# A new order of the small pieces between attention units, and a rearranged start, in a kernel that is attention times a gated MLP

## The chip, the cores and the metric

One NeuronCore of a Trainium2 chip, one launch. The metric is the time on the device in microseconds (us). Lower is better.

## The reference

All tensors are bf16; S = 2048 tokens, D = 1024, 32 heads of 32, F = 3584.

```python
xn  = layernorm(x)                                # (x - mean) / sqrt(var + 1e-5)
s   = attention(xn @ wqkv, 32 heads) @ wo         # softmax over 2048 keys
y   = layernorm(xn)
g   = silu(gelu_tanh(y @ w1 + b1) @ w2 + b2)
out = x + s * g
```

## The kernel before

The main work is 512 *attention units*. One unit takes 4 heads, 256 keys and 256 queries: scores on TensorE, two exponentials of 128x1024 on ScalarE, and P times V (with a row sum beside it) on TensorE, one unit later. From unit 7 on every unit also gets one piece of *other* work for TensorE from a hand-ordered list, `PLAN`:

```python
PLAN = """
q a a v a a a . a v a v a v a a a q a q a q a v q v a a a a q a a q ...   # 517 entries
"""
# a   w1 for 128 of F, one chunk of tokens (352 or 320 wide), 8 rounds; gelu follows
# wN  w2 for 128 of D, 28 rounds, cut into N parts (N entries); silu follows
# q   K or Q projection for a later head group, 8 rounds of 352 or 320
# v   V projection, 8 rounds of 256      o   wo, 8 rounds      .   nothing
```

A round is four matmuls side by side on four 32-column strips of the array (in the trace of the kernel before they start 3 to 4 ns apart). The loop, cut:

```python
while u < NU + LAG or ...:                 # NU = 512, LAG = 1, NP = 8
    if u < NP:  pro_unit(u)                # the prologue's projections for pair u
    if u < NU:  s_unit(u)                  # 8 score matmuls, K=32, row-tiled
    fill_act(u)                            # a tanh, if one is ready and there is room (or it is old)
    if u < NU:  exp_unit(u)                # 2 ACTIVATE Exp, 128x1024 each
    if LAG <= u < NP:  pv_unit(u - LAG)
    if u >= NP - 1 and ...:                # one PLAN entry
        for s in it.steps[lo:hi]: s(bank)
        ...
    if NP <= u < NU + LAG:  pv_unit(u - LAG)
    ...
```

The gelu of two neighbouring `a` pieces has one common tanh on ScalarE (128 x 704 or 640). `fill_act` puts it between exponentials, so some units hold two exponentials and some hold two exponentials and a tanh.

Before that stands the prologue. It normalises the 16 tiles of x (128 tokens each), transposes tiles 0 to 5 on TensorE and tiles 6 to 15 by DMA, and computes K, Q and V of the first head group for one pair of tiles per unit:

```python
def rstd(lo, hi):
    op("vector", ... tensor_scalar_add(L(0), mv[:, lo:hi, 1], EPS))        # var + eps
    op("gpsimd", ... tensor_tensor(L(2), L(0), mhalf, op=ALU.pow))         # ^ -0.5
def nbias(lo, hi):
    op("vector", ... scalar_tensor_tensor(L(3), mv[:, lo:hi, 0], -1.0, L(2), mult, mult))
def xnorm(tb):
    op("vector", ... tensor_scalar(xnb[i], x_tile, L(2), L(3), op0=mult, op1=add))

def warm(e):
    for i in range(9):                      # products with the identity: only to keep TensorE busy
        e.matmul(bank(0), lhsT=ident[:], rhs=cold, ...)                    # 128x128 by 512
for p in range(3): norm_pair(p)
transp(0); transp(1)

def pro_unit(p):
    if p + 3 < NP:  norm_pair(p + 3)
    if p >= 1:      ynorm_pro(p - 1)        # second norm of a tile, on ScalarE
    ...
    if 4 <= p < 8:  load_sub(0, p - 4)      # first w1 weights
    pair_kq(p)                              # 16 matmuls, two copies on ScalarE
    for t in (2*p + 2, 2*p + 3):
        if t < TDMA: transp(t)              # TDMA = 6
    pair_v(p)                               # 16 matmuls, a copy on ScalarE
```

The softmax here doesn't subtract the row's maximum and nothing guards it: scores larger than these inputs give would overflow.

## Time and profile before

| | before |
|---|---|
| time, median of 3 runs (range) | 1100.58 us (1100.17 to 1102.41) |
| profiled span | 1099.4 us |
| first to last score block of the prologue | to 50.48 us (unit 7) |
| main loop, unit 7 to unit 511 | 50.48 to 1081.47 us |
| of it work of TensorE, by formula | 1016.6 us |
| of it stalls of TensorE | 14.4 us |

The formula is that of the prediction below: 0.884 us for a unit plus, for its piece, rounds x (width/2400 + 0.0025) us. (The median from one round to the next is 0.149 us at width 352, 0.136 at 320 and 0.109 at 256, which is what the formula gives.) What exceeds it between one score block and the next is called a *stall*. The views that carry this are quoted in the prediction. This is the timeline of the kernel before around unit 287, whose piece is a `v` while ScalarE has a tanh (columns: start in us, length in us, engine, line, operation, output<-input, shape, count; in brackets idle time before it and what ended it; other lines of the window are left out).

```profile
626.55 0.40 PE L846 MATMUL ps<-QT,KT 32*128 32x256 bf16 x8
...
626.75 0.85 ACT L564 ACTIVATE u<-u 128x704 f32<-128x704 f32 x1
...
626.87 1.06 PE L394 MATMUL ps<-wq,xnT 128*32 128x256 bf16 x32
...
628.57 0.40 PE L846 MATMUL ps<-QT,KT 32*128 32x256 bf16 x8 [0.20 <-ACT P L858]
```

From score block to score block it is 628.57 - 626.55 = 2.02 us. TensorE's own work with a `v` is 0.884 + 8 x (256/2400 + 0.0025) = 1.757, so 0.26 us are a stall. The bracket shows 0.20 of it at the score block, put down to the exponential that had to clear its bank; the rest lies in smaller waits within the unit. The tanh has cost ScalarE 0.67 us on top of the 1.835 of two exponentials, and TensorE's piece was the shortest there is.

### The profile page before, as it was taken

To read this page: it belongs to the slowest core of one execution; us is meant where nothing else is said; L and a number is where in the kernel's file an instruction comes from. 1 tells how busy PE (TensorE), PEld (TensorE's weight loads), DVE (VectorE), ACT (ScalarE), POOL (GpSimd) and SP (SyncE) were. 2 spreads that over 40 slices of the span, in tenths; PEclk is the share of its full clock that TensorE was granted. 3 is DMA by queue.
4 is the path that set the end of the run, shared out by engine and by line. 5 is a ranking of instruction groups with operands and counts; after the bars stand their busy time and mean duration, and the time that the engine had idled before them with its cause. 6 is when DMAs were issued, how large, how long until landed. Compare 5 with 4: busy or idle time off the path is not lost.

```text
span 1099.4 us, 61736 instructions
## 1 busy us (share of the span) xinstructions
PE 1079.8 (98%) x29114; PEld 701.5 (64%) x29114; DVE 630.4 (57%) x1413; ACT 1043.8 (95%) x1192; POOL 20.1 (2%) x63
## 2 busy tenths in 40 slices
PE   7999999999999999999999999999999999999998
PEld 5766666666666666666666666666666666666665
DVE  8478853477742477642277843378732477625546
ACT  5799999899998999999999999999999999989994
POOL 2400000000000000000000000000000000000000
PEclk8999999999999999999999999999999999999999
DMA  7844447323373224342433345434244325495433
GB/s 230 164 136 148 131 112 197 92 80 109 90 179 96 72 80 132 94 103 79 132 88 118 107 100 150 119 89 127 62 114 134 90 80 147 130 263 114 105 99 108
DMA packets 209192, 131.92 MB, mean 120 GB/s; under 512 B 52522, under 2 KB 199978, under 8 KB 208938
## 3 DMA queue, kind: packets, MB, share of 16 engines
q1 hardware_dynamic: 208938, 127.97, 42.6%
q8 instruction: 228, 3.74, 1.4%
q14 instruction: 26, 0.21, 0.1%
HBM read 104.87 MB, written 12.06 MB: 106 GB/s over the span
## 4 chain that ended last, share of the span: by engine, by line
PE 54%; ACT 43%; DMA 1%; DVE 1%; SPq 0%; issue 0%; DVEq 0%
ACT P L858 39%; PE ps L394 32%; PE ps L846 9%; PE ps L875 5%; PE ps L878 5%; ACT u L564 4%; PE ps L682 1%; PE ps L698 1%; DMA xnT<-gT_scratch 0%; SPq L623 0%; ACT thz L608 0%; DMA OT<-in_A_x_dram 0%; DVE stats L322 0%; PE ps L385 0%; DVE wq L665 0%
## 5 line engine op out<-in xcount | busy, mean ns | idle before, releaser
L858 ACT ACTIVATE P<-ps 128x1024 bf16<-128x1024 f32 x1024 | 970.3, 1077 | 16.2 <-PE ps L846 10.8
L875 PE MATMUL ps<-P,VP 128*32 128x256 bf16 x4096 | 256.8, 273 | 1.3 <-ACT P L858 1.3
L878 PE MATMUL ps<-P,ones 128*32 128x256 bf16 x4096 | 256.7, 273 | 0.0
L394 PE MATMUL ps<-hT,war 128*32 128x352 bf16 (+1 forms) x5376 | 225.5, 309 | 1.0 <-DVE wq L665 0.9
L394 PE MATMUL ps<-yTc,war 128*32 128x352 bf16 (+1 forms) x5376 | 225.6, 309 | 0.2 <-issue 0.2
L846 PE MATMUL ps<-QT,KT 32*128 32x256 bf16 x4096 | 203.4, 273 | 7.4 <-ACT P L858 4.4
L394 PEld LDWEIGHTS ps<-hT,war 128*32 128x32 bf16 x5376 | 127.9, 96 | 75.4 <-issue 26.9
L394 PEld LDWEIGHTS ps<-yTc,war 128*32 128x32 bf16 x5376 | 127.6, 96 | 74.7 <-DVE xb L547 17.9
L604 DVE TENSOR_SCALAR zh<-ps,b2h 128x352 f32<-128x352 f32 (+1 forms) x48 | 27.5, 572 | 192.8 <-PE ps L394 192.8
L846 PEld LDWEIGHTS ps<-QT,KT 32*128 32x128 bf16 x4096 | 60.7, 92 | 120.2 <-issue 64.5
L547 DVE TENSOR_SCALAR xb<-ps,b1T 128x352 f32<-128x352 f32 (+1 forms) x168 | 96.2, 572 | 51.5 <-PE ps L394 47.5
L875 PEld LDWEIGHTS ps<-P,VP 128*32 128x32 bf16 x4096 | 109.8, 97 | 22.9 <-issue 1.5
L878 PEld LDWEIGHTS ps<-P,ones 128*32 128x32 bf16 x4096 | 109.9, 97 | 18.3
L570 DVE SCALAR_TENSOR_TENSOR hT<-u,xb 128x352 bf16<-128x352 f32 (+1 forms) x168 | 84.4, 509 | 63.3 <-ACT u L564 63.2
L394 PE MATMUL ps<-xnT,wq 128*32 128x352 bf16 (+1 forms) x2688 | 112.6, 309 | 0.0
L394 PEld LDWEIGHTS ps<-xnT,wq 128*32 128x32 bf16 x2688 | 63.8, 96 | 37.1 <-DVE xb L547 10.1
L557 DVE SCALAR_TENSOR_TENSOR u<-u,xb 128x352 f32<-128x352 f32 (+1 forms) x168 | 82.6, 509 | 1.6
L553 DVE TENSOR_TENSOR u<-xb 128x352 f32<-128x352 f32 (+1 forms) x168 | 82.4, 508 | 0.7
L564 ACT ACTIVATE u<-u 128x704 f32<-128x704 f32 (+1 forms) x84 | 71.0, 848 | 0.0
L394 PE MATMUL ps<-xnT,OT 128*32 128x352 bf16 (+1 forms) x1536 | 63.2, 309 | 0.2 <-DVE wq L665 0.2
L890 DVE COPY accs<-ps 128x256 f32<-128x256 f32 x64 | 26.9, 420 | 41.9 <-PE ps L878 41.8
L394 PE MATMUL ps<-wq,xnT 128*32 128x256 bf16 x1536 | 50.8, 274 | 0.0
(52 smaller groups left out, 488.4 us busy)
## 6 DMA issues: line engine op xcount, KB each, us to landing
war<-in_B_w_dram SPq DMA_DIRECT2D x336, 256.0 KB, 3.4
wq<-in_A_wqkv_dram SPq DMA_DIRECT2D x36, 128.0 KB, 2.8
OT<-in_A_x_dram SPq DMA_DIRECT2D x16, 256.0 KB, 5.2
xnT<-in_A_x_dram SPq DMA_DIRECT2D x16, 256.0 KB, 3.8
out_dram<-wq SPq DMA_DIRECT2D x16, 256.0 KB, 2.3
y_scratch<-OT SPq DMA_DIRECT2D x14, 256.0 KB, 2.5
gT_scratch<-gst SPq DMA_DIRECT2D x32, 88.0 KB, 3.2
xnT<-in_A_wo_dram SPq DMA_DIRECT2D x8, 256.0 KB, 4.5
```

The source lines that it names most:

```text
L394: ins = e.matmul(outs(j), lhsT=lhs(j), rhs=rhs, start=start, stop=stop, tile_position=(0, 32 * j), skip_group_check=True)
L547: x0 = op("vector", lambda e: e.tensor_scalar(xb[:, 0:n], bank(bk, 0, n), b1T[:, f:f + 1], None, op0=ALU.add), r=[("b", bk), "b1"], w=[kx] ...
L553: x = op("vector", lambda e: e.tensor_tensor(ub[:, 0:n], xb[:, 0:n], xb[:, 0:n], op=ALU.mult), r=[kx], w=[ku], c=151 + 1.042 * n)
L557: x = op("vector", lambda e: e.scalar_tensor_tensor(ub[:, 0:n], ub[:, 0:n], 1.0 / 0.044715, xb[:, 0:n], op0=ALU.add, op1=ALU.mult), r=[kx, ...
L564: x = op("scalar", lambda e: e.activation(ut[:, :, 0:n], ut[:, :, 0:n], ACT.Tanh, scale=0.7978845608028654 * 0.044715), r=kus, w=kus, c=48 ...
L570: op("vector", lambda e: e.scalar_tensor_tensor(hT[:, fq, 0:n], ut[:, i, 0:n], 1.0, xq[:, 0:n], op0=ALU.add, op1=ALU.mult), r=[kus[i], kq] ...
L604: x0 = op("vector", lambda e: e.tensor_scalar(zh[:, 0:n], bank(bk, 0, n), 0.25, b2h[:, nb:nb + 1], op0=ALU.mult, op1=ALU.add), r=[("b", bk ...
L846: ins = e.matmul(bank(bks[j], kh * 256, (kh + 1) * 256), lhsT=KT[i2][32 * j:32 * j + 32, k0:k0 + 128], rhs=QT[i2][32 * j:32 * j + 32, qb * ...
L858: op("scalar", lambda e, p=p, sl=sl: e.activation(pb[:, 2 * p:2 * p + 2, :, :].rearrange("p a b q -> p (a b q)"), ps[:, sl * 1024:(sl + 1) ...
L875: e.matmul(bankq(ACC, j, 0, QW), lhsT=VP[vp][:, kb, vo + 32 * j:vo + 32 * j + 32], rhs=pb[:, j, kh, :], start=first, stop=False, tile_posi ...
L878: ins = e.matmul(bankq(ACC, j, QW, 2 * QW), lhsT=ones[:, 0:32], rhs=pb[:, j, kh, :], start=False, stop=last, tile_position=(0, 32 * j), sk ...
L890: op("vector", lambda e: e.tensor_copy(a[:], bank(ACC, 0, QW)), r=[("b", ACC)], w=[ka], c=425.0)
```

## The change

The intent: fewer stalls from a better order of the pieces, and an earlier start. The order holds the same pieces, one idle entry fewer early on. The start: the identity products go from 9 to 24 and are spread around the first transposes, so that TensorE's clock does not fall back (in the trace of the kernel before it is at 0.50 from 8.76 to 15.59 us); the norm takes mean and rstd directly instead of a bias operand; V of pair 0 goes ahead of the transposes of tiles 2 and 3; ScalarE's second norm comes a unit later; the first w1 weights are loaded two units earlier.

```diff
 PLAN = """
-q a a v a a a . a v a v a v a a a q a q a q a v q v a a a a q a a q a a q a v a q a q a q v a a q w3 ...
+q a a a a q a a q a q v a a a q q a a v v a a a v v a a a a a a a q v a a q v a a a a q q q w2 q v w4 ...
 """
         def rstd(lo, hi):
-            op("vector", lambda e: e.tensor_scalar_add(L(0), mv[:, lo:hi, 1], EPS), ...)
+            op("gpsimd", lambda e: e.tensor_scalar(L(0), mv[:, lo:hi, 1], EPS, None, op0=ALU.add), ...)
             op("gpsimd", lambda e: e.tensor_tensor(L(2), L(0), mhalf[:, 0:hi - lo], op=ALU.pow), ...)
-        def nbias(lo, hi): ...
-        def xnorm(tb, eng="vector"):
-            ... e.tensor_scalar(xnb[i], x, lnp[:, 2, tb:tb+1], lnp[:, 3, tb:tb+1], op0=ALU.mult, op1=ALU.add)
+        def xnorm(tb):
+            ... e.tensor_scalar(xnb[i], x, mv[:, tb, 0:1], lnp[:, 2, tb:tb+1], op0=ALU.subtract, op1=ALU.mult)
 # ynorm likewise; its bias is now computed for two pairs only; stat(hi) goes ahead of xnorm for p = 1 too
-        def warm(e):
-            for i in range(9):
+        def warm(e, k):
+            for i in range(k):
-        transp(0)
-        transp(1)
+        for k, after in ((18, None), (1, 0), (5, 1)):
+            op("tensor", lambda e, k=k: warm(e, k), r=["ident"], w=[("b", 0)], c=("full", k, 512))
+            if after is None: transp(0)
+            elif after == 0:  transp(1)
         def pro_unit(p):
-            if p >= 1:
-                ynorm_pro(p - 1)
+            if p >= 2:
+                ynorm_pro(p - 2)
-            if 4 <= p < 4 + 4:
-                load_sub(0, p - 4)
+            if 2 <= p < 2 + 4:
+                load_sub(0, p - 2)
             pair_kq(p)
+            if p == 0:
+                pair_v(p)
             for t in range(2 * p + 2, 2 * p + 4):
                 if t < TDMA:
                     transp(t)
-            pair_v(p)
+            if p:
+                pair_v(p)
```

More of the change, by code (lines that the diff above doesn't have):

```diff
@@ L13 @@
 PLAN = """
-q a a v a a a . a v a v a v a a a q a q a q a v q v a a a a q a a q a a q a v a q a q a q v a a q w3 w4 w3 w4 v w4 w2 w2 w2 a a v a q v v a q q a a a a a q a q a a q a a v a q a v a q a a q a a a q a a v a a q q v a a w3 q w4 w4 v w3 v q v w2 w3 w3 v w4 a v v a q q q a a a a q a a a q a a q v q a a a a v q a q a q a a a v a a q a q v q a v q a v a q a q q a w3 w3 q q q v w5 q v w4 q w3 w4 w4 w2 a a a v v a a a a q a q q v a a q a v q a q a a a a q a a a a a a q v a a a a v a v q a v q q w3 w4 w4 q w4 w4 v v w4 w3 w4 a a q q q a a a v a v a a a a a a v q a a v a a a a a a a v a q q q a a a a q q v q a v v a q w3 q w4 w4 q w4 w4 w4 w4 w4 a a a a q q a a q a a q a a a q a q a q a a a a a q a a a q a q a a a a a a q w2 w4 w3 w4 o w3 o o o o w4 o o o o o o o o o o o o w3 o o o o o o o o o o o o o w4 o o o o o o o o o o o o o . o o . o o o
+q a a a a q a a q a q v a a a q q a a v v a a a v v a a a a a a a q v a a q v a a a a q q q w2 q v w4 w4 w2 w2 q v w2 q w4 w4 a a a a a q q a v q a a a a a v v q a q a a v a q q a v a a a a v a q a q q v a a a a a a w2 v w4 q w4 w2 w4 w4 w4 w3 a v a q a a v q q q a q v a q a a v a q q a a q a q a v q a a a v v a a a a q q q v a q a a q a q a q v a v a q a w3 w4 q q q w4 w3 v w4 w3 w4 w3 q v a v v a a a v a a a v q a a a a q v a a v v q a a v q a a v q a a a q a q a a a v q a a a q a w3 w4 w4 w4 w4 q v q q w4 w4 w3 a a a v a q a a a q a q a q a a a v a a a a q a a v a a v q a q a a q a a q q q v v a v a a w2 q v w4 w4 q w5 w3 q q w4 w4 w4 a a a a a q a a q a a a a a a q a q a a a q a a a q q a a q a q a a a a a w2 w4 w3 w4 w3 o o o o o o o o o o w4 o o o o o o o o o o o o w4 o o w4 o o o o o o o o o o o o o o o o o o o o o o . o o .
 """
@@ L328, in rstd @@
             L = lambda k: lnp[:, k, lo:hi]
-            op("vector", lambda e: e.tensor_scalar_add(L(0), mv[:, lo:hi, 1], EPS), r=[("mv", t) for t in range(lo, hi)],
-               w=[("l0", t) for t in range(lo, hi)], c=169.0)
+            op("gpsimd", lambda e: e.tensor_scalar(L(0), mv[:, lo:hi, 1], EPS, None, op0=ALU.add), r=[("mv", t) for t in range(lo, hi)],
+               w=[("l0", t) for t in range(lo, hi)])
             op("gpsimd", lambda e: e.tensor_tensor(L(2), L(0), mhalf[:, 0:hi - lo], op=ALU.pow), r=[("l0", t) for t in range(lo, hi)] + ["mhalf"],
                w=[("l2", t) for t in range(lo, hi)], c=708.0)
-        def nbias(lo, hi):
-            L = lambda k: lnp[:, k, lo:hi]
-            op("vector", lambda e: e.scalar_tensor_tensor(L(3), mv[:, lo:hi, 0], -1.0, L(2), op0=ALU.mult, op1=ALU.mult),
-               r=[("mv", t) for t in range(lo, hi)] + [("l2", t) for t in range(lo, hi)], w=[("l3", t) for t in range(lo, hi)], c=107.0)
         def ycoef(b):
@@ L345, in ycoef @@
             op("gpsimd", lambda e: e.tensor_tensor(L(4), L(4), L(2), op=ALU.mult), r=[("l4", b)] + l2k, w=[("l4", b)])
-            op("gpsimd", lambda e: e.tensor_scalar(L(4), L(4), 1.0, EPS, op0=ALU.mult, op1=ALU.add), r=[("l4", b)], w=[("l4", b)])
+            op("gpsimd", lambda e: e.tensor_scalar(L(4), L(4), EPS, None, op0=ALU.add), r=[("l4", b)], w=[("l4", b)])
             op("gpsimd", lambda e: e.tensor_tensor(L(5), L(4), mhalf[:, 0:2], op=ALU.pow), r=[("l4", b), "mhalf"], w=[("l5", b)], c=760.0)
@@ L348, in ycoef @@
             op("gpsimd", lambda e: e.tensor_tensor(L(6), L(2), L(5), op=ALU.mult), r=[("l5", b)] + l2k, w=[("l6", b)])
-            op("gpsimd", lambda e: e.tensor_tensor(L(7), L(3), L(5), op=ALU.mult), r=[("l5", b)] + [("l3", t) for t in range(lo, hi)], w=[("l7", b)])
-        def xnorm(tb, eng="vector"):
+            if b < 2:
+                op("gpsimd", lambda e: e.tensor_tensor(L(7), mv[:, lo:hi, 0], L(6), op=ALU.mult), r=[("l6", b)] + mvk, w=[("l7", b)])
+                op("gpsimd", lambda e: e.tensor_scalar(L(7), L(7), -1.0, None, op0=ALU.mult), r=[("l7", b)], w=[("l7", b)])
@@ L352, in xnorm @@
+        def xnorm(tb):
             i = tb % NXN
-            rk = [("xst", tb), ("l2", tb), ("l3", tb)]
-            if eng == "vector":
-                op("vector", lambda e: e.tensor_scalar(xnb[i], xst[:, tb * D:(tb + 1) * D], lnp[:, 2, tb:tb + 1], lnp[:, 3, tb:tb + 1],
-                                                       op0=ALU.mult, op1=ALU.add), r=rk, w=[("xnb", i)], c=545.0)
-            else:
-                op("scalar", lambda e: e.activation(xnb[i], xst[:, tb * D:(tb + 1) * D], ACT.Identity, bias=lnp[:, 3, tb:tb + 1],
-                                                    scale=lnp[:, 2, tb:tb + 1]), r=rk, w=[("xnb", i)], c=903.0)
+            op("vector", lambda e: e.tensor_scalar(xnb[i], xst[:, tb * D:(tb + 1) * D], mv[:, tb, 0:1], lnp[:, 2, tb:tb + 1],
+                                                   op0=ALU.subtract, op1=ALU.mult), r=[("xst", tb), ("mv", tb), ("l2", tb)], w=[("xnb", i)], c=545.0)
@@ L361, in ynorm @@
         def ynorm(tb):
             xt = xst[:, tb * D:(tb + 1) * D]
-            op("vector", lambda e: e.tensor_scalar(xt, xt, lnp[:, 6, tb:tb + 1], lnp[:, 7, tb:tb + 1], op0=ALU.mult, op1=ALU.add),
-               r=[("xst", tb), ("l6", tb // 2), ("l7", tb // 2)], w=[("xst", tb)], c=540.0)
+            op("vector", lambda e: e.tensor_scalar(xt, xt, mv[:, tb, 0:1], lnp[:, 6, tb:tb + 1], op0=ALU.subtract, op1=ALU.mult),
+               r=[("xst", tb), ("mv", tb), ("l6", tb // 2)], w=[("xst", tb)], c=540.0)
@@ L712, in norm_pair @@
                 for t in (0, 1):
-                    nbias(t, t + 1)
                     xnorm(t)
@@ L718, in norm_pair @@
             else:
-                if 1 < p < NP - 1:
+                if p < NP - 1:
                     stat(hi)
-                nbias(lo, hi)
                 for t in (lo, lo + 1):
@@ L726, in norm_pair @@
                 if p + 1 < NP:
-                    if p == 1:
-                        stat(hi)
                     stat(hi + 1)
@@ L734, in bass_recurrent_scan__mha_block__mixer_channel_mlp__prompt_kernel @@
         cold = ident[:].rearrange("p (a n) -> p a n", a=1).to_broadcast((128, 4, 128))
-        def warm(e):
-            for i in range(9):
+        def warm(e, k):
+            for i in range(k):
                 ins = e.matmul(bank(0), lhsT=ident[:], rhs=cold, start=True, stop=True, skip_group_check=True)
             return ins
-        op("tensor", warm, r=["ident"], w=[("b", 0)], c=("full", 9, 512))
         for p in range(3):
             norm_pair(p)
-        transp(0)
-        transp(1)
+        for k, after in ((18, None), (1, 0), (5, 1)):
+            op("tensor", lambda e, k=k: warm(e, k), r=["ident"], w=[("b", 0)], c=("full", k, 512))
+            if after is None:
+                transp(0)
+            elif after == 0:
+                transp(1)
         def pro_unit(p):
```

## The prediction

> **What bounds the kernel now.** I read the page first, then the waits, then two single units of the main loop, then the first 25 us microsecond by microsecond.
>
> ```profile
> PE 1079.8 (98%) x29114; PEld 701.5 (64%) x29114; DVE 630.4 (57%) x1413; ACT 1043.8 (95%) x1192; POOL 20.1 (2%) x63
> PE 54%; ACT 43%; DMA 1%; DVE 1%; SPq 0%; issue 0%; DVEq 0%
> ```
>
> Two engines, TensorE and ScalarE, are near full, and the chain that ended last changes between them. One unit is the scores of 4 heads, two exponentials, P times V, and one piece of other work on TensorE (`a` = w1, `w` = w2, `q`, `v`, `o`). What a unit costs each engine comes from the timeline and the chain:
>
> ```profile
> 556.62 0.12 PEld L846 LDWEIGHTS ps<-QT,KT 32*128 32x128 bf16 x8 [0.21 <-ACT P L858]
> 558.70 0.12 PEld L846 LDWEIGHTS ps<-QT,KT 32*128 32x128 bf16 x8 [0.21 <-issue]
> 253.05 7.33 ACT P L858 x8
> 261.05 5.50 ACT P L858 x6
> ```
>
> 556.62 to 558.70 is one unit with an `a` of width 352: 2.07 us on TensorE. Others in the same view are 1.97 (width 320) and 1.75 (width 256). So a unit is 0.88 us plus rounds x (width/2400 + 0.0025) us. ScalarE: 7.33/8 = 0.917 us for one exponential, 1.835 for the two of a unit; 253.05 to 261.05 is 8.00, so a tanh over two `a` pieces adds 0.67 (0.61 at width 320).
>
> With these I went through the 504 intervals between successive score blocks, from 50.48 us (unit 7) to 1081.47 us (unit 511): they add up to 1031.0 us, and the formula gives 1016.6. No interval falls short of the formula by more than 0.012. So **only 14.4 us of the main loop are stalls of TensorE**; the rest is work that stays. The waits agree:
>
> ```profile
> PEld ps L846 <- issue: 64.5, 305, 0.2
> PEld ps L846 <- ACT P L858: 55.3, 204, 0.8
> PE ps L846 <- ACT P L858: 4.4, 16, 0.4
> ```
>
> 0.21 is in every unit, also where nothing is waited for; 55.3 - 204 x 0.21 leaves 12.5 us for ScalarE.
>
> The prologue (to 50.48) is the other part:
>
> ```profile
> 1.38 4.02 PE L738 MATMUL ps<-ident 128*128 128x512 bf16 x9 [1.38 <-DVE ident L309]
> 7.00 0.55 DVE L355 TENSOR_SCALAR hT<-OT,lnp 128x1024 bf16<-128x1024 bf16 x1
> 7.60 0.62 PE L385 MATMUL ps<-ident,hT 128*128 128x128 bf16 x8 [2.20 <-DVE hT L355]
> 10.37 3.57 PE L682 MATMUL ps<-xnT,wq 128*128 128x256 bf16 x16 [1.21 <-ACT xnT L388]
> 13.73 1.91 PE L385 MATMUL ps<-ident,hT 128*128 128x128 bf16 x16
> 21.62 1.92 PE L698 MATMUL ps<-wq,xnT 128*128 128x256 bf16 x16 [1.12 <-ACT QT L688]
> 24.35 1.92 PE L682 MATMUL ps<-xnT,wq 128*128 128x256 bf16 x16
> ```
>
> The same 16 matmuls take 3.57 us at 10.37 and 1.92 at 24.35. Stretches of 1 us show why; the number after the five engines is the granted clock:
>
> ```profile
> 8.00:9.00 1.00, 0.81 (x12) 0.53 (x9) 1.00 (x3) 0.74 (x1) 0.00 (x0) 0.88 1.13 337
> 9.00:10.00 1.00, 0.16 (x2) 0.00 (x0) 0.96 (x3) 1.00 (x2) 0.00 (x0) 0.50 1.15 348
> 15.00:16.00 1.00, 1.00 (x12) 0.93 (x10) 0.99 (x2) 1.00 (x2) 0.00 (x0) 0.70 1.06 397
> ```
>
> Half clock from about 8.8 to 15.6 us. After that the prologue repeats every 4.48 us (score blocks at 23.47, 27.95, 32.43) with TensorE full, so time won before 23.47 is kept.
>
> [...]
>
> **The change, part by part.**
>
> *Identity products, 9 to 24* (18, then 1 between the two transposes, then 5). At 0.427 us cold the first 9 take 1.38 to 5.2. [...] the other 9 run at 0.216, to about 7.2, just before the first normalised tile at 7.3. Then 8 transposes (0.45), 1 product, 8 transposes, 5 products (1.08) fill TensorE to about 9.8[...]. The first K and Q projection, from about 10.1, takes 1.75 instead of 3.4: about 1.65 us off the path.
>
> *Norm without bias.* It takes off DVE the add of eps (0.15 to 0.17 us, 9 times, to POOL) and the bias (0.10 to 0.16, 9 times). Ahead of the first normalised tile stand two adds and a bias that DVE did between 5.11 and 7.00; POOL's add (some 0.25 us, estimated from its L346 row) runs beside the second statistics. DVE is free of the second aggregate at 6.70 instead of 7.00: 0.25 us off the path. In the main loop the tile scaling keeps its 0.54 us: nothing.
>
> *V of pair 0 ahead of the transposes of tiles 2, 3.* Before, TensorE did K and Q to 13.94, transposes to 15.64, V to 17.44. Now it has K and Q to 11.9, V to 13.6 while tiles 2 and 3 are normalised (ready 13.0 to 14.0; 12.9 and 13.4 before), then 0.9 of transposes. ScalarE copies them 14.3 to 16.3 (0.97 each), and K, Q of pair 1 starts at 16.3 (17.69 before). *The first ScalarE norm (1.25 us) moved a unit later* leaves ScalarE after the first exponentials free for the K, Q copies: 18.2 to 18.8 instead of 20.90 to 21.5, which V of pair 1 waited for (1.12 in the line above). V of pair 1 runs 18.9 to 20.6; the second score block comes at about 20.7 to 21.2 instead of 23.47. Sum of the prologue: 2.3 to 2.8 us on paper. I count 2.2[...]: at worst 18 cold products end at 9.1 and take 1.5 back.
>
> *New order.* I counted both plans: 168 `a`, 84 `q`, 48 `v`, 48 `o`, w2 with the same rounds, 517 entries; 504 of the entries before unit 511 are pieces, one more than before, as the idle entry early on is gone. Work on TensorE is the same to the round. Only the 14.4 us can move. Per unit TensorE minus ScalarE is -0.09 for `a` at 352, -0.17 at 320, -0.08 for `v`, and +0.24 for `q` at 352, +0.13 at 320. Summed from each chunk's first `a` to its first `w`, ScalarE needs more in all six, old: 1.5, 0.5, 1.9, 0.7, 0.7, 2.5 = 7.8 us; new: 0.7, 1.0, 1.6, 1.4, 0.7, 2.9 = 8.3. That part stays. The other 6.6 are single events: 0.65 at the idle entry; 2.85 from 970 to 989 us around the first loads and the first `o`; the rest bunches of `v`. The new plan drops the first, has its last `q` six units earlier, so xnT is free for the wo and gate loads some 12 us earlier, and has five instead of four w2 pieces before the first `o`. I give it 2 of the 6.6.
>
> Sum: 1100.6 - 2.2 - 2.0 = 1096.4; I say 1096.
>
> **Rivals.** (1) *The order gains more*, all 6.6 us: 1092. For it: a plan that was searched; against: the old one was too, and ScalarE's deficits are not smaller in the new one. (2) *V's weights come too late*: they are 2.62 MB down the queue, and the bytes per microsecond add up to 2.46 MB at 10 and 2.78 at 11 us, so they land near 10.5 if in order, against 11.9 needed; interleaved with the x tiles behind them it could be 13 to 16, and the prologue gain shrinks to 1: 1097.5. (3) *Cold products delay the first transposes* by up to 1.5 us and the clock is still warm later: 1097.5. (4) *The statistics of tile 4 now stand ahead of normalising tile 2* and wait for its x (some 11.3 us): costs at most 0.5. (5) *The new order stalls more*, say 4 us, by weights not landed or bunched tanh: 1100.
>
> **Range and chances.** Most of the time is fixed work, so the range is narrow: prologue 0.5 to 3.5 us, order -1.5 to +6. That makes 1092 to 1099.5. 2% is 22 us; the stalls of the whole main loop are 14.4, and with the prologue's best 3.5 that is 17.9. Faster by over 2%: 0.02; within: 0.97; slower: 0.01.
>
> **What would show it.** The clock row without 0.50 after the first 5 to 8 us; the 16 matmuls of the first K and Q projection in about 1.9; second score block near 21; last score block of the prologue near 48 instead of 50.48; the 4.48 us period unchanged; about 1029 from there to the last score block, instead of 1031. I would be wrong if the projection at 10 us were still at half clock, if V of pair 0 waited for a DMA, or if the stalls after 50 us changed by more than 6 us either way.

Cut from it, where marked, are one paragraph and three clauses, on what makes the granted clock rise and fall and in which order transfers are taken, which no trace of this case shows. No term of the sum went with them: it came to 1100.6 - 2.2 - 2.0 = 1096.4. But that the last 9 of the first 18 products run at the full rate, and that the clock then stays up, stands in it as my estimate only, and with it the 1.65 us for the first projection. The rates themselves are in the trace of the kernel before: 0.427 us from product to product at the start, and 16 matmuls 0.213 us apart at clock 0.50 (3.4 us) and 0.109 at 1.00 (1.75). The 0.216 is the formula's for 512 columns, and what the kernel after shows.

## The result, and the profile after

| | before | after |
|---|---|---|
| time, median of 4 runs (range) | 1100.38 (1099.37 to 1102.41) us | 1093.93 (1093.07 to 1094.82) us |
| ratio, with 95% interval | | 0.9939 (0.9922 to 0.9956) |
| profiled span | 1099.4 us | 1091.3 us |
| second score block (unit 1) | 23.47 us | 21.39 us |
| last score block of the prologue (unit 7) | 50.48 us | 49.30 us |
| score block of unit 511 | 1081.47 us | 1073.33 us |
| stalls from unit 7 to unit 511 | 14.39 us | 7.43 us |

A ratio here is the mean time of one kernel's runs over that of the other's runs of the same rounds, so it is not quite the ratio of the medians that stand beside it. The change is faster by 0.6%: within the 2% that was predicted. The two profiles differ by 8.1 us: 1.18 up to the last score block of the prologue and 6.96 in the main loop; the end (17.95 us after the last score block in both) is the same. The medians differ by 6.45, because the profiled run of the new kernel was its fastest (1093.07) and that of the old (1101.21) lay above its median.

The page of the kernel after, engines and the chain that ended last:

```profile
PE 1079.6 (99%) x29129; PEld 701.6 (64%) x29129; DVE 628.0 (58%) x1395; ACT 1041.3 (95%) x1192; POOL 22.4 (2%) x68
...
PE 54%; ACT 43%; DVE 2%; DMA 1%; SPq 0%; issue 0%
```

TensorE is busy for the same time to 0.2 us: the 15 additional products stand against matmuls that no longer run at half clock (the first projection took 3.57 us and takes 1.91). What moved is waiting, not work. The waits of the kernel after (total us, times, longest us):

```profile
PEld ps L840 <- issue: 61.3, 289, 0.5
PEld ps L840 <- ACT P L852: 53.7, 219, 0.8
...
PE ps L840 <- ACT P L852: 0.6, 2, 0.4
```

0.21 us stands ahead of every score block. Less that, waiting for the exponentials is 53.7 - 219 x 0.21 = 7.7 us; the same sum was 12.5 before. The 4.4 us of matmuls that waited for an exponential are 0.6 now. So the main loop lost fewer microseconds to ScalarE, though ScalarE has the same exponentials and tanh.

The start of the kernel after, from the timeline:

```profile
1.38 6.72 PE L726 MATMUL ps<-ident 128*128 128x512 bf16 x18 [1.38 <-DVE ident L309]
...
8.38 0.38 PE L726 MATMUL ps<-ident 128*128 128x512 bf16 x1
9.04 1.24 PE L726 MATMUL ps<-ident 128*128 128x512 bf16 x5
...
10.66 1.91 PE L674 MATMUL ps<-xnT,wq 128*128 128x256 bf16 x16 [0.38 <-ACT xnT L380]
...
12.22 1.29 DVE L322 BATCH_NORM_STATS2 stats<-OT 128x6 f32<-128x512 bf16 x2 [1.07 <-DMA OT<-in_A_x_dram]
12.40 1.91 PE L690 MATMUL ps<-wq,xnT 128*128 128x256 bf16 x16
...
21.39 0.40 PE L840 MATMUL ps<-QT,KT 32*128 32x256 bf16 x8
...
32.15 1.92 PE L674 MATMUL ps<-xnT,wq 128*128 128x256 bf16 x16 [0.85 <-DMA xnT<-hT]
```

The first projection (10.66) takes 1.91 us instead of 3.57: full clock. V of pair 0 follows at once (12.40), with no wait for its weights. The second score block is 2.08 us earlier than before. And then, at 32.15, a projection waits 0.85 us for a DMA, where TensorE was full before. The clock by microsecond (after the five engines' busy shares: granted clock, DMA share, GB/s; ahead of the first record of the clock, at 6.79 us in this run, the column shows 1.00 although the first products run at half rate, 0.427 us apart and later 0.216):

```profile
8.00:9.00 1.00, 1.00 (x18) 0.88 (x17) 1.00 (x3) 0.42 (x1) 0.00 (x0) 1.00 1.14 346
9.00:10.00 1.00, 1.00 (x9) 0.43 (x6) 0.96 (x3) 1.00 (x2) 0.00 (x0) 1.00 1.17 354
```

The stretch 9 to 10 was 0.16 busy and at clock 0.50 before; it is full and at 1.00 now. What the wait at 32.15 is made of stands in the chain that ended last (start, length, engine, what it made, line, count):

```profile
25.72 0.85 DVE stats L322 x2
26.57 5.53 DMA xnT<-hT
```

The chain goes through a DMA transpose of 5.53 us, that of tile 9, which lands at 32.10; the projection at 32.15 is its next step. VectorE's statistics stand before it in the chain, but it did not wait for them: tile 9 had been normalised by 25.72, and SyncE, which issues the transposes, was busy with that of tile 8 until 26.52. Is VectorE slow here, or the transpose? The kernel of run products9 (below) settles it. There tile 9 was normalised at 25.61 and its transpose issued at 26.46, both as in the kernel after (25.72, 26.57). From issue to landing this one transpose took, in the kernel after and in products9 (last number, us):

```profile
xnT<-hT SPq DMA_TRANSPOSE x1, 5.5
```

```profile
xnT<-hT SPq DMA_TRANSPOSE x1, 2.8
```

In products9 it landed at 29.27 and nothing waited for it. With 2.8 us it would have landed at 29.4 in the kernel after, 1.9 us before TensorE wanted it (31.30). So the wait is made by one slow transpose, and VectorE's pace is not what holds the prologue. While the slow one was under way the DMA engines moved 5 GB/s from 29 to 30 us, and a packet of 16,384 bytes of the kind "instruction" (queue q8 of the trace) ran inside it, from 28.52 to 29.50. All five profiles in which TensorE waits for tile 9 have such a packet inside this transpose (it starts between 28.17 and 28.65; the transpose takes 5.36 to 5.89); in products9 and v_after it starts at 29.43 and 29.13, as the transpose ends (29.27 and 29.51), and the transpose takes 2.81. That the packet makes the transpose slow is not shown, only that they meet.

**Two tables that the reasons rest on.** First, stalls in each stretch of `a` units (from a chunk's first `a` to its first `w`), in us, with what the prediction had as ScalarE's excess there:

| stretch | 1 | 2 | 3 | 4 | 5 | 6 | sum |
|---|---|---|---|---|---|---|---|
| old order, predicted | 1.5 | 0.5 | 1.9 | 0.7 | 0.7 | 2.5 | 7.8 |
| old order, measured | 2.5 | 0.28 | 2.16 | 2.18 | 1.19 | 1.63 | 9.94 |
| new order, predicted | 0.7 | 1.0 | 1.6 | 1.4 | 0.7 | 2.9 | 8.3 |
| new order, measured | 0.68 | 0.55 | 1.44 | 0.76 | 0.64 | 1.8 | 5.87 |

Second, the stalls by the kind of piece and by whether ScalarE starts a tanh of w1 in that unit (units, us; unit 7, a `q` with 0.51 in both orders, is left out):

| piece | old, no tanh | old, tanh | new, no tanh | new, tanh |
|---|---|---|---|---|
| a | 121: 0.10 | 47: 3.77 | 115: 0.00 | 53: 3.43 |
| q | 61: 0.10 | 22: 2.02 | 60: 0.04 | 23: 1.50 |
| v | 39: 0.90 | 9: 3.02 | 48: 0.92 | none |

Nearly all stalls of `a` and `q` lie in units with a tanh. A `v` with a tanh costs 0.34 us each, an `a` or `q` with one 0.07 to 0.08. Nine such `v` in the old order, none in the new. That is 3.02 of the 6.96 us. The rest of the difference: the idle entry 0.65, `a` and `q` with a tanh 0.86, the w2 and wo pieces 2.29 (3.32 to 1.03), the remainder 0.14. Of the 2.29, 0.99 is a wait behind the first `o` (old_o_later below). This is an accounting, not yet a cause; the experiments test it.

### The profile page after: what moved, and what is told of

It reads as the page before. It is cut to its first block, busy times and chain, and to the rows that moved or that the text cites. A ratio compares the mean times of both kernels' runs of the same rounds, so it can differ in the third digit from the quotient of the medians.

```text
span 1091.3 us, 61755 instructions
## 1 busy us (share of the span) xinstructions
PE 1079.6 (99%) x29129; PEld 701.6 (64%) x29129; DVE 628.0 (58%) x1395; ACT 1041.3 (95%) x1192; POOL 22.4 (2%) x68
## 4 chain that ended last, share of the span: by engine, by line
PE 54%; ACT 43%; DVE 2%; DMA 1%; SPq 0%; issue 0%
ACT P L852 39%; PE ps L386 33%; PE ps L840 9%; PE ps L869 5%; PE ps L872 5%; ACT u L556 4%; DVE stats L322 1%; PE ps L674 1%; PE ps L690 1%; DMA OT<-in_A_x_dram 1%; DMA xnT<-hT 1%; DVE hT L350 0%; ACT thz L600 0%; SPq L284 0%; SPq L274 0%
## 5 line engine op out<-in xcount | busy, mean ns | idle before, releaser
L852 ACT ACTIVATE P<-ps 128x1024 bf16<-128x1024 f32 x1024 | 968.5, 1082 | 10.5 <-PE ps L840 5.8
L386 PEld LDWEIGHTS ps<-xnT,OT 128*32 128x32 bf16 x1536 | 37.3, 96 | 21.1 <-DVE wq L657 7.7
```

What stands on the lines that cost most here:

```text
L386: ins = e.matmul(outs(j), lhsT=lhs(j), rhs=rhs, start=start, stop=stop, tile_position=(0, 32 * j), skip_group_check=True)
L852: op("scalar", lambda e, p=p, sl=sl: e.activation(pb[:, 2 * p:2 * p + 2, :, :].rearrange("p a b q -> p (a b q)"), ps[:, sl * 1024:(sl + 1) ...
```

## The experiments

All runs were right against the reference but for the two that are wrong. Kernels of one call shared one chip and the same runs of the kernel before: its medians were 1101.81, 1099.81 and 1100.04 us in the three calls. "Block 2" is the score block of unit 1, "last block" that of unit 7. With no change to the prologue the last block fell at 50.48, 51.15, 49.77 and 49.90 us in four profiles (mean 50.33), with the new prologue at 49.30, 49.10, 48.95 and 49.40 (mean 49.19).

### Each part alone

**order_only**: the kernel before with the new order alone.

```diff
 PLAN = """
-q a a v a a a . a v ...
+q a a a a q a a q a ...
```

> The kernel before with the new unit order alone. Theory (from the two traces: stalls of the main loop 14.4 us before, 7.4 after; last score block of the prologue 50.48 and 49.30): nearly all of the gain is the order, so 6 to 7 us less than before, some 1093.5, with the prologue ending at 50.5 as before. Rival, as I had predicted: the order gives 2 us, and the rest needs the new prologue (an earlier start that shifts what ScalarE and TensorE do against each other): 1098.4.

Measured: 1095.31 us, ratio 0.9935 (0.9922 to 0.9947); last block 51.15, stalls 8.27. In the times the order alone brings what the whole change brings (0.9939). The theory that the order is nearly all of it holds; its rival falls.

**prologue_only**: the kernel after with the old order.

```diff
 PLAN = """
-q a a a a q a a q a ...
+q a a v a a a . a v ...
```

> The kernel after with the old unit order. Theory: 1.2 us less than before in a run whose clock rises as in the trace of after (49.30 for the last score block), 1099.2; stalls of the main loop 14.4 us as before. Rival: 4 us or more less (1096), if the prologue had been what mattered.

Measured: 1100.21 us, ratio 0.9975 (0.9962 to 0.9988); block 2 at 22.11, last block 49.10. So the new start does help alone, by 0.25%, 1 to 4 us by the interval. Its profiled run was the slowest of its five (1103.17) and had 17.65 us of stalls where 14.4 were expected, 4.11 of them in one event at 977.7 us; the old order stalls 13.3 to 17.7 from profile to profile. The product of the two ratios is 0.9910 and the combined kernel has 0.9932 to 0.9939 in two measurements: the two parts do not add up cleanly. Whether that is more than the intervals can hold is left open. In this run V of pair 0 did wait, as the waits of prologue_only show:

```profile
PEld ps L690 <- DMA wq<-in_A_wqkv_dram: 0.4, 1, 0.4
```

V's weights landed at 12.22 us there. In the kernel after they landed at 11.41, and V's matmuls start at 12.40 without a wait, 1.0 us later.

### Inside the prologue

**products9**: the kernel after with the old 9 identity products.

```diff
-        for k, after in ((18, None), (1, 0), (5, 1)):
-            op("tensor", lambda e, k=k: warm(e, k), ...)
+        for k, after in ((9, None), (0, 0), (0, 1)):
+            if k:
+                op("tensor", lambda e, k=k: warm(e, k), ...)
```

> The kernel after with only the 9 identity products of before. Theory: the first K and Q projection runs at half clock again (3.4 us instead of 1.9), but the first transposes start 0.7 us sooner (at 7.1, not 7.9). The second score block comes 1 to 1.5 us later than the 21.39 of after, and the time is 0.5 to 1.5 us longer than after's. Rival: no loss, since the V of pair 0 and the statistics of tile 4 (waiting for x to 12.2) hide it: then the second score block is at 21.4 and the times are equal within 0.3.

Measured: 1095.36 us, ratio 0.9938 (0.9926 to 0.9950). Its timeline:

```profile
10.50 3.57 PE L674 MATMUL ps<-xnT,wq 128*128 128x256 bf16 x16 [1.21 <-ACT xnT L380]
...
23.14 0.40 PE L841 MATMUL ps<-QT,KT 32*128 32x256 bf16 x8
```

Half clock was back from 7.69 to 14.52 us, and the first projection at 3.57 us. Block 2 comes 1.75 later than in the kernel after (23.14 to 21.39), which is the clock's share as predicted (1.65). But the last block is at 50.14, only 0.84 later than in the kernel after and 0.95 later than the mean of the new starts. Half of the gain of the clock does not reach the main loop, as the kernel after loses 0.91 us to the slow transpose and products9 nothing. In the times no loss is seen at all: 0.9938 beside 0.9933 for subs_late.

**subs_late**: is the wait at 32.15 made by the w1 loads that now stand in the same queue two units earlier (theory A), or by VectorE's statistics, which hold back the DMA transposes (theory B)? The kernel after with those loads where they were:

```diff
-            if 2 <= p < 2 + 4:
-                load_sub(0, p - 2)
+            if 4 <= p < 4 + 4:
+                load_sub(0, p - 4)
```

> The kernel after with the first w1 loads issued in units 4 to 7 of the prologue again. In the trace of after the fourth K projection waits 1.1 us for a DMA transpose (it starts at 32.15), which the trace of before does not show. Theory A: the loads that now run among the DMA transposes slow them; then the wait goes and the time is 0.9 us less than after's. Theory B: the wait comes from TensorE being 2.1 us earlier while the transposes, held by DVE's statistics (its chain is full up to 26.6 us), are not: then the wait stays at about 1 us and the time is that of after within 0.3.

Measured: 1095.21 us, ratio 0.9933 (0.9920 to 0.9946), block 2 at 21.58, last block 49.25. The timeline of subs_late:

```profile
32.09 1.92 PE L674 MATMUL ps<-xnT,wq 128*128 128x256 bf16 x16 [0.60 <-DMA xnT<-hT]
```

The same projection starts at 32.09 instead of 32.15 and waits as before (0.6 on the matmuls and 0.9 on their weight loads, 0.8 and 1.1 in the kernel after). Theory A falls; the transpose of tile 9 took 5.36 us there with those loads out of the way. The wait stays, as theory B has it, but its reason does not hold: in products9 VectorE is as late, the transpose takes 2.81, and the wait is gone. What remains is the slow transpose. The six blocks after block 2 tell the same: they take 27.00 us (within 0.01) in eight of the fourteen profiles and 27.18 to 27.92 in the five that wait for tile 9 (27.42 in light_old).

**after_again**: the kernel after once more, unchanged, to see how steady its start is.

> The kernel after once more, to stand beside the others on one chip: ratio 0.993 to 0.995, stalls of the main loop 7 to 9 us, last score block of the prologue at 49.1 to 49.4 us, as tiles 8 and 9 land no sooner than about 32 us.

Measured: 1092.04 us (1091.11 to 1095.86), ratio 0.9932 (0.9918 to 0.9946); block 2 at 21.12, last block 48.95, a wait of 0.76 for a DMA transpose at 31.79; stalls 6.76 (block and stalls both a little under what was expected). The wait is there again, with a transpose of 5.54 us.

**v_after** (one look): the kernel after with V of pair 0 behind the transposes again.

```diff
             pair_kq(p)
-            if p == 0:
-                pair_v(p)
             for t in range(2 * p + 2, 2 * p + 4): ...
-            if p:
-                pair_v(p)
+            pair_v(p)
```

> The kernel after with the V of pair 0 behind the transposes of tiles 2 and 3 again. In after, TensorE has finished V of pair 0 at 14.2 when tile 2 is ready at 14.2. Without it ahead TensorE waits for these tiles from 12.4 to 14.2 and V follows at 15.2 to 17.0. Theory: first score block 1.8 us later (17.0), K and Q of pair 1 about the same (they wait for ScalarE's copies of tiles 2, 3), second score block 0.5 to 1.5 us later than 21.1 to 22.1; the last of the prologue within 0.5 us of after's 49.0 to 49.3, since tiles 8 and 9 land at 32 anyway. Rival: the whole 1.8 us shows at the last score block (51).

Measured: 1093.23 us. Timeline of v_after:

```profile
14.36 1.13 PE L377 MATMUL ps<-ident,hT 128*128 128x128 bf16 x16 [2.45 <-DVE hT L350]
15.29 3.56 PE L690 MATMUL ps<-wq,xnT 128*128 128x256 bf16 x16
...
23.78 0.40 PE L837 MATMUL ps<-QT,KT 32*128 32x256 bf16 x8
```

TensorE is idle for 2.45 us up to 14.36, while the tiles are normalised. The clock falls after it: V at 15.29 takes 3.56 us instead of 1.91. The granted clock of v_after is 0.63, 0.50, 0.50 and 0.67 in the four stretches from 15 to 19 us, where the kernel after has 1.00. Block 2 is 2.39 us later than in the kernel after and the last block (50.78) 1.48 later: at block 2 more than the 1.7 us of V, as V itself took 1.65 us longer at the lower clock. The expectation (0.5 to 1.5 at block 2, at most 0.5 at the last block) missed in both, since tile 9 landed at 29.51 here and not at 32; its rival was nearer. So V's place and the products do one job together: with both, the clock is at 1.00 from 6.79 us on (after); without the 15 products it is at half from 7.69 to 14.52 (products9), and without V ahead it falls at 15 to 16. The single time (1093.23) does not resolve 1.5 us against the spread of the kernel after (1091 to 1096).

**y_early** (one look): the kernel after with ScalarE's second norm a unit earlier, as before the change.

```diff
-            if p >= 2:
-                ynorm_pro(p - 2)
+            if p >= 1:
+                ynorm_pro(p - 1)
```

> The kernel after with ScalarE's norm of tile 0 one unit earlier again (between the first exponentials and the K, Q copies of pair 1). Theory: these copies come 1.1 us later (in before: 20.90 after the norm), V of pair 1 waits for its bank, and the second score block comes 1.1 us later than in after (22.3 to 23.2); the last of the prologue within 0.4 us of after's, because of the transposes that land at 32. Rival: no change at the second block, if ScalarE's copies of tiles 4, 5 hold it anyway.

Measured: 1091.53 us; block 2 at 21.82, last block 49.00. V of pair 1 waits again for the copies of K and Q, 0.69 us up to 19.97, where the kernel before had 1.12. Block 2 moves by 0.43, less than the expectation had, and the last block not at all: the wait for tile 9, which lands at 31.80 here too, swallows it.

### The order

**light_old** and **light_new**: the old and the new order with every exponential on 928 of its 1024 columns. The rest of P is zeroed once at the start. The results are wrong (relative error 0.110). TensorE's work stays; ScalarE has 9% fewer columns in each exponential. In light_old one takes 944 ns in the mean, busy 902.9 us in all, against 1077 ns and 970.3 us in the kernel before. If the stalls are ScalarE's lag behind TensorE, they go; if they are loads and buffers, they stay.

```diff
+        for i in range(2):
+            op("gpsimd", lambda e, i=i: e.memset(P[i][:], 0.0), w=[("P", i, 0), ("P", i, 1)])
-                    pb[...].rearrange("p a b q -> p (a b q)"), ps[:, sl * 1024:(sl + 1) * 1024], ACT.Exp, ...
+                    pb[...].rearrange("p a b q -> p (a b q)")[:, 0:928], ps[:, sl * 1024:sl * 1024 + 928], ACT.Exp, ...
```

> The kernel before, wrong on purpose: each exponential takes 928 of its 1024 columns (the rest of P is zero)[...]. Theory: 10 of the 14.4 us of stalls are waits for a lagging ScalarE and go; 3 to 5 us stay (first loads of the tail, idle entry): 10 us less, ratio 0.991. Rival: the stalls are waits for DMA and DVE: ratio above 0.997.

> The kernel after with the same lighter exponentials. If the new order gains because it keeps ScalarE from lagging, little is left to gain here (5 to 6 us, stalls 1 to 3 us), and light_old and light_new differ by 1 to 4 us only: the order's 7 us shrink to less than half. Rival (the order removes waits for DMA and DVE): the two differ by 7 us as before.

Measured: light_old 1090.02 us, ratio 0.9909 (0.9896 to 0.9922), stalls 4.98. light_new 1086.61 us, ratio 0.9875 (0.9860 to 0.9890), stalls 0.42. The waits of light_old:

```profile
ACT P L860 <- PE ps L848: 49.8, 151, 1.7
...
PEld ps L848 <- ACT P L860: 14.7, 63, 0.8
```

and those of light_new:

```profile
ACT P L854 <- PE ps L842: 40.9, 143, 1.2
...
PEld ps L842 <- ACT P L854: 5.9, 26, 0.6
```

Now ScalarE waits for TensorE, 41 to 50 us in all, and TensorE's waits for exponentials fall to 14.7 - 63 x 0.21 = 1.5 and 5.9 - 26 x 0.21 = 0.4 us. So easing ScalarE takes away some 9.4 of the old order's 14.4 us of stalls and nearly all of the new order's 7.4. Of the 4.98 that stay in light_old up to 1.5 may, by this sum, still be waits for exponentials; 4.0 are four single events: 0.57 at the idle entry, and 163.6 (1.36, TensorE waiting for a load of w2 weights, in no other profile), 865.6 (0.91) and 969 us (1.14, behind the first `o`). The profiles differ by 4.6 us with ScalarE eased, where the expectation had 1 to 4; the median times differ by 3.4, which is within it (the profiled run of light_old was its slowest, 1090.98). The new order is then cleaner in two ways, by less lag of ScalarE and by fewer single events. One blemish: zeroing P held POOL for 3.62 us at the start and shifted the prologue (last blocks 49.66 and 50.15), so the ratios of the light kernels are less exact than their stalls.

**old_o_later**: the kernel before with the first `o` one w2 item later, as the prediction had put part of the loss to the early `o`.

```diff
-... q w2 w4 w3 w4 o w3 o o o o w4 ...
+... q w2 w4 w3 w4 w3 o o o o o w4 ...
```

> The kernel before with its first output piece three w2 parts later (as the new order has it: w3 o instead of o w3). In the trace of before the first o waited for the gate's DMA and held its bank, some 1.0 to 1.3 us. Theory: this wait goes, stalls from 975 to 990 us fall by 1 us: ratio 0.999. Rival: it only moves to the next piece that needs that data: ratio 1.000.

Measured: 1099.62 us, ratio 1.0002 (0.9989 to 1.0015). Stalls 13.31. The kernel before has an event of 0.99 us at 978.8, and old_o_later one of 1.76 at 979.1, so it looks as if the event only moved, as the rival says. The traces say otherwise. First the kernel before, then old_o_later:

```profile
980.11 1.21 PEld L394 LDWEIGHTS ps<-hT,war 128*32 128x32 bf16 x40 [1.21 <-DVE wq L665]
```

```profile
981.20 1.06 PEld L394 LDWEIGHTS ps<-hT,war 128*32 128x32 bf16 x33 [1.68 <-issue]
```

In the first, a w2 piece waits until VectorE has emptied the bank of the first `o`, and VectorE waits 1.32 us for the gate's DMA, as the theory has it. That wait is in all four profiles with the first `o` at its old place (0.93, 1.07, 1.12 and, in prologue_only, 2.89 us ahead of the matmuls), and neither in old_o_later nor in any profile of the new order. So moving the `o` did take it away; 1 us in 1100 is under what the ratio resolves. The second is another event: TensorE waits for nothing that the profile names.

Such nameless waits are in both orders, mostly in the tail, and come and go from profile to profile. The kept traces show what they have in common. There are 228 of the 16,384-byte "instruction" packets in each trace, and in the kernel before TensorE has 2 x 29,114 matmuls and weight loads besides some 170 instructions of its sequencer: 256.1 to a packet. That they belong together, one packet to 256 instructions, is an estimate from these two counts. Counted in blocks of 256 along TensorE's instructions, 30 of the 31 nameless gaps of over 0.3 us ahead of a weight load in the fourteen main loops lie at the same place of a block (matmuls and weight loads alone counted from 0, it is number 193 or 194 in the kernels before and after), and 29 of these come 1.27 to 1.64 us after a packet had landed. What TensorE waits for there is not shown. Waits at this place, named or not, stand in units with 2.5 us of stalls in the kernel before, 1.2 in the kernel after and none in v_after, so by this estimate some 1.3 of the 6.96 us between the two profiles is chance. No run tested it.

**v_off_tanh**: the kernel before with six `v` swapped with a near `q`, out of units that hold a tanh (units 20, 32, 52, 200, 287, 289 with 24, 31, 51, 201, 290, 293). Nothing else moves in the list; but the program places each tanh by its own estimate of time, and eight of the 84 moved by one or two units.

```diff
-... a v a v a v a a a q a q a q a v q v a ...
+... a v a v a q a a a v a q a q a v v q a ...
```

> The kernel before with six v pieces exchanged with a q up to four units away, so that none of the six runs in a unit in which ScalarE also takes a w1 tanh (all of these six did; they stall 1.94 us together). Theory (placement): a v in a unit with a tanh stalls TensorE 0.34 us, a q in its place 0.09: stalls of the main loop fall by 1.4 us (1.2 to 1.8), at those units. Rival (the sum of a stretch decides, as I had predicted): stalls move to other units and their sum stays within 0.5 us.

Measured: 1098.47 us (1098.23 to 1099.97), ratio 0.9992 (0.9978 to 1.0006); stalls 12.01. At the six units stalls go from 1.94 to 0.12 us, at their partners from 0 to 0.46: net 1.36 less, where 1.4 was expected. (Most of the other 1.0 us of the fall is a nameless wait of 1.26 at 970.0 in the kernel before, which is absent here.) This is unit 287 in v_off_tanh, with a `q` of width 320:

```profile
624.99 0.40 PE L846 MATMUL ps<-QT,KT 32*128 32x256 bf16 x8
...
625.19 0.85 ACT L564 ACTIVATE u<-u 128x704 f32<-128x704 f32 x1
...
625.32 1.27 PE L394 MATMUL ps<-xnT,wq 128*32 128x320 bf16 x32
...
627.01 0.40 PE L846 MATMUL ps<-QT,KT 32*128 32x256 bf16 x8
```

Again 2.02 us from score block to score block, the same as with the `v`, and now without the wait: the `q` does 0.884 + 8 x (320/2400 + 0.0025) = 1.97 us of work in the time that the `v` left 0.26 unused. The 0.21 us that the `q` is longer are saved where it came from. In the time it is 0.08%, inside the interval, so the time alone does not show it; the unit-by-unit record does.

**v_on_tanh**: the reverse in the kernel after, fourteen `v` swapped onto units with a tanh.

```diff
-... a q a q v a a a q q ...
+... a q a v q a a a q q ...
```

> The kernel after with fourteen v pieces exchanged with a q that runs in a unit with a w1 tanh (in the trace of after no v does). Theory (placement): stalls grow by 2 to 4 us, at those units (fourteen times up to 0.31, less where ScalarE was ahead). Rival (sum of a stretch): within 0.5 us of after's 7 to 8 us.

Measured: 1095.72 us (1094.26 to 1098.55), ratio 0.9963 (0.9950 to 0.9976); stalls 10.12. At the fourteen units stalls go from 0.78 to 2.88 us. Only ten of the fourteen `v` met a tanh, as the tanhs moved here too; these ten cost 0.22 each. Against after_again (0.9932) this is 0.3% slower. It was run at another time. There were two costs on top of it: a nameless wait of 0.55 at 155.4 us, and 1.85 at 303.5, where a w2 part waited for a gelu whose tanh came late:

```profile
307.14 0.77 PE L386 MATMUL ps<-hT,war 128*32 128x352 bf16 x8 [1.38 <-DVE hT L562]
```

So where `v` and tanh meet is a cause in both directions, by about 0.22 us a time (1.36 for six, 2.25 for ten). It does not make up the whole of the order's gain: 1.4 of about 7 us was moved by it in v_off_tanh, 3.0 is its share in the accounting.

### What was not run

A kernel before with its idle entry taken out could not be built: a `q` fell outside the units in which its input and output buffers are free. The idle entry's 0.65 us is therefore only read from profiles (0.56 to 0.68 in all five of the old order; 0.57 is left of it in light_old, so it is not ScalarE's). No run was clearly faster than the kernel after: subs_late, y_early and after_again lie within its own spread.

## Why the prediction was right or wrong

The prediction, 1096.0 with 1092.0 to 1099.5 and "within 2%" at 0.97, held: 1093.93, and 1092.04 in the second measurement. But its two terms were off in opposite directions: prologue -2.2, order -2.0 predicted; -1.1 and -7 to -8 measured. The order gained more than the most that was allowed for it (6), and that the sum stayed in the range is in part luck.

**The bound: right.** TensorE's formula gives 1016.6 us in both orders, busy time is the same to 0.2 us, and light_new, with ScalarE eased, has 0.42 us of stalls. The stalls were what could move, and little else.

**Identity products: right in kind, and in size at block 2** (products9: 1.75 us, predicted 1.65). The clock row has no 0.50 after the first microseconds. Two details differ. The products were still at 0.427 us after the first 9, and the rise came at about 6.8: 18 products at 0.427 and then 0.216 us, from 1.38 to the first transpose at 7.93, give that time (the first record of the clock, at 1.00, begins at 6.79; in the kernel before at 5.35), and from run to run they took 5.63 to 6.93 us. What sets the time of the rise is not shown. So the first transposes began at 7.93 instead of 7.60, a small form of the third rival, and the gain of the norm without bias (tile 0 normalised from 6.41 instead of 7.00, 0.59 rather than the 0.25 predicted) was hidden behind the products.

**V of pair 0 ahead: right**, and worth more than I gave (v_after), since without it TensorE idled for 2.45 us and the clock was at 0.50 from 16 to 18 us. V's weights landed at 11.41 in the kernel after and 12.22 in prologue_only, not at 10.5, and V waited 0.4 for them there. The second rival was nearer than I thought. That the loads land in order was an assumption. The bytes per microsecond were not all that the trace gave: it has each load's landing, and in the kernel before V's weights landed at 11.56. The fourth rival happened too: the statistics of tile 4 waited 1.07 us for x, which landed at 12.22 rather than 11.3.

**ScalarE's norm a unit later: right at V of pair 1** (y_early: the wait is back with 0.69), nothing at the end of the prologue.

**"TensorE full, so time won before 23.47 is kept": wrong.** Block 2 came 2.08 earlier, near what I had (2.2). Then 0.9 to 1.1 us were lost at 32 us, because the DMA transpose of tile 9 landed at 32.10. The period of 4.48 us did not hold there. I had read "TensorE full" as if nothing else could hold it. With the 2.81 us that it took in products9 and v_after this transpose would have a margin of about 2 us; it took 5.53 (and 5.22 in the kernel before, where TensorE came later and did not wait). Where the transpose was quick, in products9 and v_after, the period held. The last block, predicted near 48, is at 49.30.

**The order: the step that failed.** It reads: "Summed from each chunk's first `a` to its first `w`, ScalarE needs more in all six ... 7.8 us; new ... 8.3. That part stays." It did not stay: 9.94 us became 5.87, and the new order is at or below the supposed floor in all six stretches, the old order in two. The sum treated ScalarE's excess over a stretch as lost time, whatever the order within it. (Redone with the prediction's own costs per unit, and without the idle entry, the sums are 7.8 and 9.0; the new order's floor was too low by 0.7, which makes the miss larger.) What the runs showed in its place is that stalls sit where pieces and tanh meet: `a` and `q` units without a tanh stall by 0.2 us in 182 units in the old order, a `v` with a tanh by 0.34 each, an `a` or `q` with one by 0.07 to 0.08. v_off_tanh took 1.36 us off by six swaps, v_on_tanh put 2.1 us on by fourteen, with the same sums of work in nearly the same stretches. Why the measured stalls can be below the sum at all was not tested; that ScalarE carries its lag beyond the first `w` into units with room is my reading only.

**The single events: right in the main.** I gave the order 2 of 6.6 us outside the stretches; there stalls fell from 4.45 to 1.56, by 2.9. The idle entry went (0.65), and so did the wait behind the first `o` (0.99); the other profiles show the same. The remaining 1.2 or so is no property of the order as far as the traces show: nameless waits come and go in both. In light_old, too, 1.7 of the 4.0 us of single events are these two. Why the order's and the prologue's gains do not add up in the times stays open.

By its own criterion, "if the stalls after 50 us changed by more than 6 us either way", the prediction's account of the order is refuted (6.96 here; by means over all profiles with the normal exponentials, 15.1 in three of the old order and 7.3 in seven of the new, before any swap of `v`). The first rival, all 6.6 us for 1092, was nearer in size and not in mechanism: it too left the 7.8 us of the stretches in place, and 4.1 us of the gain came from there.

## What to carry to other kernels

When two engines are both near full, compare them unit by unit and not by sums over stretches: the same work, ordered so that the short piece of one engine never meets the long piece of the other, had half the stalls here. An engine that looks "full" for a few periods may hide a second chain with little margin; before a gain is said to be kept, look for the next thing that the following steps wait for, and at its slowest case, not its usual one (here a transpose that took 2.81 us in two profiles and 5.53 in the kernel after). When an event is gone and another of the same size stands near its place, compare what each waits for before calling it the same. And work that does nothing but keep the clock up may pay only in part: the 15 products were worth 1.75 us at the second score block and 0.84 at the last, since another bound came next, and with them in place but 2.45 us idle further on (v_after) the clock fell all the same.
